# Key-value products of two linear-attention branches moved into one burst behind the first denominators

## The chip, the cores and the metric

One Trainium2 chip, one core. The metric is device microseconds of one execution; the median of several timed executions is compared. A profile is one further execution, recorded instruction by instruction.

## What is computed

```
g = sigmoid((x * gate_w).sum(-1))                   # x: 2048 x 640
for each branch (A, B), with its own wqkv, wo, 32 heads of 20:
    q, k, v = split(x_A @ wqkv)
    phi(t) = where(t > 0, t + 1, exp(t)) + 1e-6
    kv = einsum("bhsd,bhse->bhde", phi(k), v);  z = phi(k).sum(s)
    o  = (phi(q) @ kv) / (phi(q) @ z + 1e-6)
    branch = o @ wo
out = g * A + (1 - g) * B
```
Both branches read the same x. Matrix operands are bf16, sums fp32.

## The kernel before

Instead of forming v, the kernel uses that kv = phi(k)^T (x wv) = (phi(k)^T x) wv. It works in these steps.

- **Keys** (`k_both`, lines 531 to 578): 16 tiles of 128 tokens, both branches; phi is an exponential on ACT (ScalarE) and two VectorE instructions; the results PK fill the buffer FE.
- **G** (`g_unit`, 582 to 610): per branch five units of 32 matmuls, G = phi(k)^T x with the row sums z; ACT copies each to GS, a DMA transposes it into GT.
- **The m step** (`m_unit`, 622 to 656): per branch 55 small matmuls (128 rows, 64 columns of the array, at two column positions in turn) form G wv for groups of heads in one PSUM bank. Three VectorE multiplications ("masks", line 647) keep only the blocks of a head with itself and write MB.
- **W' units** (`wp_unit`, 658 to 682): kv times wo, so that value and output projections become one 640 x 640 matrix a branch. Eleven in all: five for A, five for B, and one that does the last 40 rows of both. Each is two matmuls into a pair of adjacent PSUM banks and one eviction to WS. Of A's, three evictions are on VectorE (line 680) and two on ACT; the other six are on ACT (682).
- **Rows** (`wp_store`, `wp_rows`, 684 to 698): WS goes to DRAM (wrowsA, wrowsB) and back into WPA and WPB with the rows reordered. SP issues these DMAs and those of the factors and outputs, in one queue.
- **Queries** (`q_unit`, 724 to 756): four blocks of 512 tokens, ten units each (A 0 to 4, B 0 to 4). A unit is five matmuls of 512 columns into one bank, an exponential on ACT (743), and on VectorE a min (747) and a max-and-add (752), called the two halves of a query below. They end in PQ, which lies in the same buffer FE.
- **Denominators** (`dens`, 758): phi(q) z for two blocks at once, 20 matmuls at four column positions of 32. `scale_q` (781) copies them with ACT (DN, "dn0", "dn1"), takes reciprocals on VectorE (793, "rc0", "rc1", 1.74 us each), writes them to DRAM and reads them back spread over partitions (RX), and multiplies PQ by them (811, "ML").
- **Finals** (`final`, 822): per 128 tokens and branch ten matmuls of 320 columns, PQ times WPA or WPB, joined with the gates and stored.

In the program the order is: keys; G of A; gates; G of B with A's m step after the second unit and A's W' units between the later ones; block 0 queries; B's m step; block 1 queries with the six remaining W' units between them (`WPLAG`, line 28, sets how many query units one comes later); the rows of W'; denominators 0 (blocks 0 and 1); blocks 2 and 3; denominators 2; finals.

The order on each engine is not that of the program. `_Sched.schedule` (136) is a planner that runs once, when the kernel is built. It simulates the five engines with fixed costs: a query unit 1079 ns on TensorE, halves 201 and 601 ns, `_dve_ns` (291) 380 ns for a large mask, 1740 ns for a reciprocal, and 180 to 190 ns from the end of an operation until another that depends on it may start. At each point it takes the operation that can start first; among those within 20 ns it takes the one that stands first in the program. A ready operation that stands late therefore fills any gap, and nothing is put aside for one that becomes ready a little later. The planner also assigns the eight PSUM banks, the one free longest first; a tile of two banks needs both banks of an even-odd pair (`place`, 153). On the chip every engine then runs its list strictly in order, with waits on semaphores wherever `plan` (226) finds a dependency that isn't implied by an earlier one, reuse of a bank included. Successive VectorE readers of one PSUM tile, such as the masks, count as dependent on each other (lines 103 and 115).

Of the kernel before, what the change touches and what calls it, by code (L numbers as in the profile page):

```python
# [15 lines left out]
ACT = mybir.ActivationFunctionType  # L16
# [3 lines left out]
D = 640  # L20
H = 32
DH = 20
NT = 16
NB = 4
NC = 5
EPS = 1e-6
HALF = 320
WPLAG = 2
XW = 672
# [54 lines left out]
class _Sched:  # L84
# [141 lines left out]
    def plan(self):  # L226
# [7 lines left out]
        for o in sorted(self.ops, key=lambda o: (o.start, o.idx)):  # L234
# [19 lines left out]
            for d in waits.values():  # L254
                for f in ENGINES:
                    k[f] = max(k[f], d.know[f])
            o.waits = list(lean.values())
            used.update(d for d in o.waits if d.sem is None)
# [28 lines left out]
def _act_ns(n, psum=True):  # L287
    return n / 1.2 + (52.0 if psum else 94.0)


def _dve_ns(n, rate=1):
    return n / (0.96 * rate) + 68.0
# [6 lines left out]
def bass_gated_mix__linear_attn_block__linear_attn_block__prompt_kernel(nc, A_x, A_wqkv, A_wo, B_x, B_wqkv, B_wo, gate_w, out):  # L299
# [6 lines left out]
    with ExitStack() as es:  # L306
        E = es.enter_context

        def sb(name, shape, dtype=dt.bfloat16):
            return E(nc.sbuf_tensor(name, shape, dtype))  # L310
# [13 lines left out]
        W5 = sb("W5", [128, D])  # L324
        MB = sb("MB", [128, 6, 120])
        WS = sb("WS", [120, 6, D])
# [79 lines left out]
        sch.op("POOL", lambda e: e.memset(W5[:, :], 0.0), 500, writes=[("W5", X) for X in XS], name="w5z")  # L406
        sch.op("POOL", lambda e: e.memset(MB[:, :, :], 0.0), 700, writes=[("M", q) for q in range(6)], name="mz")
        def load_x(eng, t):
# [212 lines left out]

        def m_unit(X):

            tile = _Tile(1)
            last = XS.index(X)

            def steps():
                r = []
                for q in range(6):
                    w = 12 if q < 5 else 8  # L630
                    for j in range(NC):
                        for g in (0, 1) if q < 5 else (last,):
                            at = D * j + 120 * q + 60 * g * (q < 5)
                            r.append((
                                PS[64 * g : 64 * g + 64, tile.banks[0], 60 * q : 60 * q + NC * w], WV[X][:, at : at + 64],
                                GT[X][:, j, :, 24 * q + 12 * g * (q < 5) : 24 * q + 12 * g * (q < 5) + w], j == 0, j == NC - 1, (0, 64 * g),
                            ))
                return r

            mms("m%s" % X, steps, [("GT", X, k) for k in range(NC)] + [("WV", X), ("WVP", X)], [(tile,)], 25 * 75 + 400)  # L640
            for q0, q1, g, w in ((0, 5, 0, 12), (0, 5, 1, 12), (5, 6, last, 8)):
                n = DH * (w // 4)

                def mask(e, q0=q0, q1=q1, g=g, w=w, n=n):
                    p0 = 64 * g
                    m = CB[p0 : p0 + n, C_MM : C_MM + 60].rearrange("p (k i) -> p k i", i=12)[:, :, 0:w]
                    return e.tensor_tensor(
                        out=MB[p0 : p0 + n, q0:q1, 60 * g : 60 * g + n].rearrange("p q (i k) -> p q k i", k=NC),
                        in0=PS[p0 : p0 + n, tile.banks[0], 60 * q0 : 60 * q0 + n * (q1 - q0)].rearrange("p (q k i) -> p q k i", k=NC, i=w),
                        in1=m.unsqueeze(1).to_broadcast([n, q1 - q0, NC, w]), op=ALU.mult,  # L650
                    )

                sch.op(
                    "DVE", mask, _dve_ns(n * (q1 - q0)), reads=[(tile,), ("CB",)], writes=[("M", q) for q in range(q0, q1)],
                    name="mm%s" % X,
                )

        def wp_unit(X, q):

            tile = _Tile(2)  # L660
            w = W5 if q == 5 else WO[X][:, q, :]

            def steps():
                return [
                    (PS[0:120, tile.banks[h], 0:HALF], MB[0:124, q, :], w[0:124, HALF * h : HALF * h + HALF], True, True, None)
                    for h in (0, 1)
                ]

            mms(
                "wp%s%d" % (X, q), steps, [("M", q)] + [("W5", Y) for Y in XS if q == 5] + [("WO", X, g) for g in (0, 1) if q < 5],  # L670
                [(tile,)], D + 60,
            )
            dst = WS[:, q, :].rearrange("p (h f) -> p h f", f=HALF)

            def src():
                return PS[0:120, tile.banks[0] : tile.banks[1] + 1, 0:HALF]

            name = "wpe%s%d" % (X, q)
            if X == "A" and q % 2 == 0:
                sch.op("DVE", lambda e: e.tensor_copy(dst, src()), _dve_ns(D), reads=[(tile,)], writes=[("WS", q)], name=name)  # L680
            else:
                sch.op("ACT", lambda e: e.activation(dst, src(), ACT.Copy), _act_ns(D), reads=[(tile,)], writes=[("WS", q)], name=name)

        def wp_store(X):
            dma(
                "SP", "ws" + X, WD[X].ap()[0:600, :].rearrange("(q p) f -> p q f", p=120), WS[:, 0:5, :], reads=[("WS", q) for q in range(5)],
                writes=[("WD", X, 0)], us=2.0,
            )

        def wp_rows(X):  # L690

            nat = WD[X].ap()
            p0 = 60 * XS.index(X)
            dma("SP", "ws5" + X, nat[600:D, :], WS[p0 : p0 + 40, 5, :], reads=[("WS", 5)], writes=[("WD", X, 5)], us=0.2)
            dma(
                "SP", "wp" + X, WP[X][:, :, :], nat.rearrange("(i k) f -> i k f", k=NC), reads=[("WD", X, 0), ("WD", X, 5)],
                writes=[("WP", X, k) for k in range(NC)], us=2.2,
            )
# [59 lines left out]
        def dens(b0):  # L758
# [3 lines left out]
            def den():  # L762
# [11 lines left out]

            mms(
                "den%d" % b0, den, [("ZBD", X) for X in XS] + [("PQ", X, k, b) for X in XS for k in range(NC) for b in (b0, b0 + 1)],
                [(dtile,)], 5 * 540,
            )
            return dtile

# [120 lines left out]
        gates()  # L901
        g_unit("B", 0)
        g_unit("B", 1)
        m_unit("A")
        g_unit("B", 2)
        for q in (0, 1):
            wp_unit("A", q)
        g_unit("B", 3)
        for q in (2, 3):
            wp_unit("A", q)  # L910
        g_unit("B", 4)
        wp_unit("A", 4)
        wp_store("A")
        zbd("B")
        def queries(b):
            for X in XS:
                for k in range(NC):
                    q_unit(X, b, k)
                    q = 5 * (X == "B") + k - WPLAG
                    if b == 1 and 0 <= q < 6:  # L920
                        wp_unit("B", (q - 1) % 6)
                        if q == 0:
                            wp_rows("A")

        def finals(b):
# [5 lines left out]

        queries(0)
        m_unit("B")
        queries(1)
        wp_store("B")
        wp_rows("B")
        d01 = dens(0)
        scale_q(0, d01, 2)
        queries(2)
        queries(3)  # L940
        scale_q(1, d01, 2)
        d23 = dens(2)
        finals(0)
# [38 lines left out]
```

## Time and profile before

| | us |
|---|---|
| median of three timed runs | 190.35 (190.13 to 191.41) |
| the profiled execution's own time | 190.84 |
| its span, first to last instruction | 189.5 |
| TensorE busy / VectorE / ScalarE | 186.2 / 130.2 / 76.5 |
| A's m step, B's m step start at | 79.56, 105.98 |
| first query matmul | 95.09 |
| first denominators, second denominators | 121.77, 146.59 |
| first final | 142.42 |

Times in the profile count from the start of the span. A line of a group gives source line, engine, operation, output and inputs by tile name, shapes, count, then the busy time in us and the mean duration in ns, then the idle time ahead of it and who ended it. Consecutive matmuls overlap, so the distance of their starts, not their duration, is what one costs TensorE. In the views PEld is the load of the stationary operand, DVE is VectorE, ACT is ScalarE and SPq the issue of a DMA by SP.

### The profile page before, as it was taken

The page shows a single profiled execution, that of the slowest core. Times are in us where ns is not written, and L with a number is a line of the kernel's source. Part 1 is how long each engine was busy: PE and PEld are TensorE (multiplying, and loading weights), DVE is VectorE, ACT ScalarE, POOL GpSimd, SP SyncE. Part 2 cuts the span into 40 slices and gives each one's busy share as a digit, 9 for nine tenths or more (in the row PEclk, how much of TensorE's full clock was granted, in tenths as well). Part 3 has the DMA queues.
Part 4 walks back from the last instruction along what each step waited for, and adds up shares of the span by engine and source line. Part 5 has one row for each costly group of instructions (what it writes and reads, how often), then busy time and mean ns, then how long its engine had stood idle before and what let it go on. Part 6 is the DMA issues. An engine that isn't in the chain of part 4 may idle for free.

```text
span 189.5 us, 3208 instructions
## 1 busy us (share of the span) xinstructions
PE 186.2 (98%) x1289; PEld 124.2 (66%) x1289; DVE 130.2 (69%) x275; ACT 76.5 (40%) x129; POOL 8.2 (4%) x14
## 2 busy tenths in 40 slices
PE   8999999999999999999999999999999999999995
PEld 3555555555788888888855666455556677777774
DVE  1498988898600009996179997899999959833324
ACT  2255656565311112203255478565553422332332
POOL 8900000000000000000000000000000000000000
DMA  5999799991011111111143005675000173221212
GB/s 191 289 230 193 171 390 365 355 246 42 0 35 38 35 35 38 35 35 38 35 90 107 5 22 173 162 227 171 0 0 3 50 222 91 98 72 39 73 69 69
DMA packets 31936, 21.49 MB, mean 113 GB/s; under 512 B 16818, under 2 KB 31666, under 8 KB 31922
## 3 DMA queue, kind: packets, MB, share of 16 engines
q1 hardware_dynamic: 31490, 20.80, 39.9%
q10 hardware_dynamic: 432, 0.49, 0.7%
q8 instruction: 10, 0.16, 0.4%
q14 instruction: 4, 0.03, 0.1%
HBM read 12.05 MB, written 5.31 MB: 92 GB/s over the span
## 4 chain that ended last, share of the span: by engine, by line
PE 94%; DMA 3%; SPq 1%; issue 0%; ACT 0%; DVE 0%
PE ps L383 94%; DMA WK<-in_B_wqkv_dram 3%; SPq L372 1%; ACT TS L859 0%; DVE OL L865 0%
## 5 line engine op out<-in xcount | busy, mean ns | idle before, releaser
L383 PE MATMUL ps<-WK,XT 128*128 128x512 bf16 (+2 forms) x250 | 44.2, 337 | 0.4 <-DMA WK<-in_B_wqkv_dram 0.4
L383 PE MATMUL ps<-XN,FE 128*128 128x320 bf16 x320 | 44.3, 300 | 0.0
L383 PEld LDWEIGHTS ps<-XN,FE 128*128 128x128 bf16 x320 | 37.5, 117 | 6.0
L383 PEld LDWEIGHTS ps<-WK,XT 128*128 128x128 bf16 x250 | 24.1, 98 | 19.9 <-DMA WK<-in_B_wqkv_dram 1.1
L743 ACT ACTIVATE EK<-ps 128x512 bf16<-128x512 f32 x40 | 23.9, 597 | 18.4 <-PE ps L383 17.9
L563 ACT ACTIVATE EK<-ps 128x512 bf16<-128x512 f32 (+1 forms) x42 | 21.4, 526 | 16.2 <-PE ps L383 16.2
L752 DVE SCALAR_TENSOR_TENSOR FE<-ps,EK 128x512 bf16<-128x512 f32 x40 | 26.8, 687 | 0.7
L859 ACT ACTIVATE TS<-ps,GA 128x640 f32<-128x640 f32 (+2 forms) x18 | 13.2, 734 | 29.6 <-PE ps L383 29.6
L383 PE MATMUL ps<-WPB,FE 128*128 128x320 bf16 (+1 forms) x165 | 24.7, 295 | 0.0
L383 PE MATMUL ps<-WPA,FE 128*128 128x320 bf16 (+1 forms) x165 | 24.7, 295 | 0.0
L573 DVE SCALAR_TENSOR_TENSOR FE<-ps,EK 128x512 bf16<-128x512 f32 (+1 forms) x42 | 23.9, 597 | 0.5
L865 DVE SCALAR_TENSOR_TENSOR OS<-ps,GA,TS 128x640 bf16<-128x640 f32 x15 | 13.0, 868 | 15.2 <-PE ps L383 12.8
L383 PE MATMUL ps<-XT,WQA 128*128 128x512 bf16 x100 | 22.8, 380 | 0.0
L383 PE MATMUL ps<-XT,WQB 128*128 128x512 bf16 x100 | 22.7, 379 | 0.0
L600 ACT ACTIVATE GS<-ps 128x640 bf16<-128x640 f32 x10 | 7.0, 704 | 37.1 <-PE ps L383 37.1
L383 PEld LDWEIGHTS ps<-WPA,FE 128*128 128x128 bf16 x165 | 15.9, 98 | 6.1
L383 PEld LDWEIGHTS ps<-WPB,FE 128*128 128x128 bf16 x165 | 15.8, 98 | 6.2 <-ACT TS L859 0.4
L383 PEld LDWEIGHTS ps<-XT,WQB 128*128 128x128 bf16 x100 | 11.7, 117 | 9.2
L383 PEld LDWEIGHTS ps<-XT,WQA 128*128 128x128 bf16 x100 | 11.6, 118 | 9.4 <-issue 0.4
L705 DVE SCALAR_TENSOR_TENSOR GP<-XN,GWB 128x640 bf16<-128x640 bf16 x16 | 13.2, 828 | 4.1 <-PE ps L383 3.6
L567 DVE TENSOR_SCALAR EK<-EK 128x512 bf16<-128x512 bf16 (+1 forms) x42 | 11.4, 271 | 3.1
L811 DVE TENSOR_TENSOR FE<-FE,RX 128x1280 bf16<-128x1280 bf16 (+1 forms) x20 | 12.6, 684 | 1.1 <-DMA RX<-factor 1.1
(52 smaller groups left out, 81.1 us busy)
## 6 DMA issues: line engine op xcount, KB each, us to landing
out_dram<-OS SPq DMA_DIRECT2D x15, 160.0 KB, 1.8
XN<-in_A_x_dram SPq DMA_DIRECT2D x3, 640.0 KB, 8.5
factor<-RC SPq DMA_DIRECT2D x4, 256.0 KB, 2.6
RX<-factor SPq DMA_DIRECT2D x4, 256.0 KB, 3.1
WVA<-in_A_wqkv_dram SPq DMA_DIRECT2D x1, 800.0 KB, 10.3
WQA<-in_A_wqkv_dram SPq DMA_DIRECT2D x1, 800.0 KB, 11.7
WVB<-in_B_wqkv_dram SPq DMA_DIRECT2D x1, 800.0 KB, 11.2
WQB<-in_B_wqkv_dram SPq DMA_DIRECT2D x1, 800.0 KB, 12.3
```

What stands on the lines that cost most here:

```text
L372: ins = e.dma_start(dst() if callable(dst) else dst, src() if callable(src) else src, transpose=transpose)
L383: ins = pe.matmul(o, l, r, start=a, stop=z, tile_position=tp, skip_group_check=True)
L563: "ACT", lambda e, ps=ps, ek=ek: e.activation(ek(), ps(), ACT.Exp), _act_ns(n), reads=[(tile,)], writes=[(es,)],
L567: "DVE", lambda e, ek=ek: e.tensor_scalar(ek(), ek(), 1.0, EPS, op0=ALU.min, op1=ALU.add), _dve_ns(n, 4),
L573: return e.scalar_tensor_tensor(out=out, in0=two(ps()), scalar=0.0, in1=two(ek()), op0=ALU.max, op1=ALU.add)
L600: "ACT", lambda e: e.activation(GS[:, k, :].rearrange("p (h f) -> p h f", f=HALF), pair(tile, HALF), ACT.Copy),
L705: lambda e, t=t: e.scalar_tensor_tensor(out=GP[:, :], in0=XN[:, t, 0:D], scalar=1.0, in1=GWB[:, :], op0=ALU.mult, op1=ALU.mult, accum_out= ...
L743: "ACT", lambda e: e.activation(ek(), PS[:, tile.banks[0], :], ACT.Exp), _act_ns(512), reads=[(tile,)],
L752: lambda e: e.scalar_tensor_tensor(out=dst, in0=PS[:, tile.banks[0], :], scalar=0.0, in1=ek(), op0=ALU.max, op1=ALU.add),
L811: return e.tensor_tensor(out=v, in0=v, in1=RX[:, xs.slot, 512 * x + w * j : 512 * x + w * j + w].unsqueeze(1).to_broadcast([128, NC, w]), ...
L859: "ACT", lambda e, acc=acc, t_ap=t_ap: e.activation(t_ap(), acc(), ACT.Copy, scale=GA[:, 0, t : t + 1]),
L865: lambda e, acc=acc, t_ap=t_ap, o_ap=o_ap: e.scalar_tensor_tensor(out=o_ap(), in0=acc(), scalar=GA[:, 1, t : t + 1], in1=t_ap(), op0=ALU.m ...
```

## The change

- A's and B's m steps become one operation, `m_both`, of 110 matmuls into two banks: A's and B's full groups, then the two 40-row remainders in turn. It is made to follow the first denominators on TensorE (`after`). Six masks follow; MB holds eleven groups instead of six.
- All eleven W' units stand among the queries of blocks 2 and 3, each WPLAG = 3 units after its place in the count, in the order A 0 to 4, the shared one, B 0 to 4. Their evictions are all on ACT. A's go to GS (free once G has been transposed), B's to WS.
- A's rows are stored and reloaded after the sixth W' unit, B's after the eleventh.
- `queries(2)` now stands ahead of `scale_q(0)`.
- Where an instruction waits for several others, the waits stand in the order of the planned ends.

```
-WPLAG = 2
+WPLAG = 3
...
-            o.waits = list(lean.values())
+            o.waits = sorted(lean.values(), key=lambda d: d.end)
...
-        MB = sb("MB", [128, 6, 120])
+        MB = sb("MB", [128, 11, 120])
...
-        def m_unit(X):
+        def m_both(after):
+            tiles = [_Tile(1), _Tile(1)]
+            def step(x, q, g, j):
+                w, lo = (12, 12 * g) if q < 5 else (8, 0)
+                at = D * j + 120 * q + DH * lo // 4
+                return (
+                    PS[64 * g : 64 * g + 64, tiles[x].banks[0], 60 * q : 60 * q + NC * w], WV[XS[x]][:, at : at + 64],
+                    GT[XS[x]][:, j, :, 24 * q + lo : 24 * q + lo + w], j == 0, j == NC - 1, (0, 64 * g),
+                )
             def steps():
+                r = [step(x, q, g, j) for x in (0, 1) for q in range(5) for j in range(NC) for g in (0, 1)]
+                return r + [step(x, 5, x, j) for j in range(NC) for x in (0, 1)]
+            mms(
+                "m", steps, [("GT", X, k) for X in XS for k in range(NC)] + [("WV", X) for X in XS] + [("WVP", X) for X in XS],
+                [(t,) for t in tiles], 110 * 38 + 240, after=after,
+            )
+            for x, q0, q1, g, w in ((0, 0, 5, 0, 12), (0, 0, 5, 1, 12), (0, 5, 6, 0, 8), (1, 5, 6, 1, 8), (1, 0, 5, 0, 12), (1, 0, 5, 1, 12)):
+                n = DH * (w // 4)
+                o0 = 10 if q0 == 5 else 5 * x
...
+        def ws(u):
+            return GS[0:120, u, :] if u < 5 else WS[:, u - 5, :]
+        def wp_unit(u):
...
-            if X == "A" and q % 2 == 0:
-                sch.op("DVE", lambda e: e.tensor_copy(dst, src()), _dve_ns(D), reads=[(tile,)], writes=[("WS", q)], name=name)
-            else:
-                sch.op("ACT", lambda e: e.activation(dst, src(), ACT.Copy), _act_ns(D), reads=[(tile,)], writes=[("WS", q)], name=name)
+            sch.op(
+                "ACT",
+                lambda e: e.activation(
+                    ws(u).rearrange("p (h f) -> p h f", f=HALF), PS[0:120, tile.banks[0] : tile.banks[1] + 1, 0:HALF], ACT.Copy
+                ),
+                _act_ns(D), reads=[(tile,)], writes=[("WS", u)] + [("GS", u)] * (u < 5), name="wpe%d" % u,
+            )
...
-            return dtile
+            return dtile, o
...
-        g_unit("B", 0)
-        g_unit("B", 1)
-        m_unit("A")
...
+        for k in range(NC):
+            g_unit("B", k)
         zbd("B")
+        order = [0, 1, 2, 3, 4, 10, 5, 6, 7, 8, 9]
         def queries(b):
             for X in XS:
                 for k in range(NC):
                     q_unit(X, b, k)
+                    i = 10 * (b - 2) + 5 * (X == "B") + k - WPLAG
+                    if 0 <= i < 11:
+                        wp_unit(order[i])
+                        if i == 5:
+                            wp_store("A")
                             wp_rows("A")
+                        if i == 10:
+                            wp_store("B")
+                            wp_rows("B")
...
         queries(0)
-        m_unit("B")
         queries(1)
-        wp_store("B")
-        wp_rows("B")
-        d01 = dens(0)
+        d01, den = dens(0)
+        m_both(den)
+        queries(2)
         scale_q(0, d01, 2)
-        queries(2)
         queries(3)
         scale_q(1, d01, 2)
-        d23 = dens(2)
+        d23, _ = dens(2)
```

## The prediction

> **What bounds the kernel now.** I read the page's busy line and chain first, then the chain in order of time, then busy time by stretch.
>
> ```profile
> PE 186.2 (98%) x1289; PEld 124.2 (66%) x1289; DVE 130.2 (69%) x275; ACT 76.5 (40%) x129; POOL 8.2 (4%) x14
> ```
> ```profile
> 9.17 177.87 PE ps L383 x1241
> ```
> From 9.17 to 187.04 us TensorE hands on to itself; no other engine releases it. So the end moves by what TensorE's own sequence gains or loses, and any new wait on TensorE adds in full: there is no slack ahead of it.
>
> Busy time of the engines by stretch (PE, PEld, DVE, ACT, POOL), core 0:
>
> ```profile
> 95.10:105.90 10.80, 10.80 (x52) 5.74 (x49) 9.38 (x20) 6.06 (x10) 0.00 (x0) 1.00 0.36 86
> ...
> 119.50:131.60 12.10, 12.10 (x71) 6.24 (x70) 11.26 (x21) 6.92 (x12) 0.00 (x0) 1.00 0.70 200
> 131.60:142.40 10.80, 10.80 (x51) 5.85 (x50) 10.80 (x25) 5.97 (x10) 0.00 (x0) 1.00 0.06 18
> 142.40:152.80 10.40, 10.40 (x88) 6.92 (x87) 10.40 (x15) 3.92 (x6) 0.00 (x0) 1.00 0.18 59
> ```
> Among the block-2 and 3 queries (119.5 to 142.4) VectorE is as full as TensorE. It is late there but hidden: TensorE runs ahead through the eight PSUM banks. That is the stretch into which the change puts work. The costs, by shape:
>
> ```profile
> L752 DVE SCALAR_TENSOR_TENSOR FE<-ps,EK 128x512 bf16<-128x512 f32 x40 | 26.8, 687 | 0.7
> ...
> L793 DVE RECIPROCAL RC<-DN 128x256 bf16<-128x256 f32 x4 | 7.0, 1742 | 0.1
> ...
> L682 ACT ACTIVATE WS<-ps 120x640 bf16<-120x640 f32 x8 | 5.6, 698 | 0.0
> ...
> L647 DVE TENSOR_TENSOR MB<-ps,CB 60x300 bf16<-60x300 f32 x4 | 4.1, 1030 | 0.2
> ...
> L680 DVE CAST WS<-ps 120x640 bf16<-120x640 f32 x3 | 2.5, 822 | 5.9 <-PE ps L383 5.9
> ...
> L647 DVE TENSOR_TENSOR MB<-ps,CB 40x40 bf16<-40x40 f32 x2 | 0.5, 274 | 0.1
> ```
> A large mask takes 1.03 us; the planner (which fixes every engine's order and every bank) books 0.38. Now B's m step, in order of time:
>
> ```profile
> 100.49 5.56 PE L383 MATMUL ps<-XT,WQB 128*128 128x512 bf16 x25
> ...
> 105.98 1.13 PE L383 MATMUL ps<-GTB,WVB 128*64 128x60 bf16 x55
> ...
> 107.04 2.96 PEld L383 LDWEIGHTS ps<-XT,WQA 128*128 128x128 bf16 x15
> ...
> 107.15 1.02 DVE L647 TENSOR_TENSOR MB<-ps,CB 60x300 bf16<-60x300 f32 x1
> 107.92 0.77 DVE L752 SCALAR_TENSOR_TENSOR FE<-ps,EK 128x512 bf16<-128x512 f32 x1
> ```
> 25 query matmuls 0.216 us apart (5.40 us a block half, 1.08 a unit) end at 105.89; the next query starts at 107.04. So m costs TensorE 1.15, of which 0.09 at its entry is the change of tile shape (m starts 0.31, not 0.216, after the last query). An independent instruction follows a mask after 0.77. And the first denominators:
>
> ```profile
> 121.77 0.39 PE L383 MATMUL ps<-FE,ZBDA 128*32 128x512 bf16 x2
> ...
> 122.97 3.43 PE L383 MATMUL ps<-XT,WQA 128*128 128x512 bf16 x15
> ...
> 123.59 1.75 DVE L793 RECIPROCAL RC<-DN 128x256 bf16<-128x256 f32 x1
> 125.26 0.23 DVE L747 TENSOR_SCALAR EK<-EK 128x512 bf16<-128x512 bf16 x1
> ...
> 125.41 1.74 DVE L793 RECIPROCAL RC<-DN 128x256 bf16<-128x256 f32 x1
> ```
> First denominator matmul to first query after it: 1.20; to the first reciprocal: 1.82. A reciprocal holds VectorE 1.67 (123.59 to 125.26). The planner put the second one between the two halves of a query, because that gap was free in its plan: it fills gaps without looking ahead. This matters below.
>
> **TensorE's own work.** Removed: A's m step (79.56 to 80.61 plus 0.09 at entry, 1.15) and B's (1.15): 2.30. Added: one burst of 110 matmuls. In the trace two column halves start together and such pairs follow every 0.032; the five last ones (one half only) take 0.032 each. The burst pairs everything: 55 pairs, 1.78, plus 0.12 to the next query. Its entry switch replaces that from the denominators to queries (0.31 in either case). So 1.90, a gain of 0.40; the trace's one slow gap of 0.03 behind each switch back goes once more: **0.45**. The eleven W' units keep their price: 117.08 to 117.36 is 0.28, wherever they stand. Bounds: 0.35 (no pairing gain) to 0.55 (no drain between the two column shapes).
>
> [...]
>
> **What moves with it.** Without m and five W' units in A's share (1.15 + 5 x 0.27 = 2.5) queries start at 92.6 instead of 95.1; block 0 and 1 lose 1.15 + 6 x 0.28 more, so the denominators start 26.7 - 2.85 later, at D = 116.4. With eighteen query units, burst and eleven W' units behind D, TensorE would be through the queries at 142.0 (before: 142.4). VectorE loses three W' evictions (3 x 0.82), all from a stretch where it had room (9.6 of 15.6 us busy from 79.5 to 95.1); worth nothing. ACT gains them: a query plus a W' eviction is 0.60 + 0.70 against 1.36 of TensorE, and the rows of 111 to 118 show ACT keeping up at just that mix. [...] The sum takes ACT.
>
> The larger zero fill of MB (0.70 x 11/6 = 1.28 on POOL near 7 us) delays two fills that nothing needs before 52 us: nothing. Sorted waits: the trace has 25 separate wait records of 51 ns on TensorE's queue, under cover today. At most three waits will really be late, so within 0.15 either way; I take 0.
>
> **The new wait.** Six masks now stand behind D instead of at 81 and 107: VectorE has no slack there. The order follows from the planner's own costs (used for order only; times are the trace's). Its mask chain is serial with 0.18 us between links, so rc1 fills the first gap: rc0, mask 1, rc1, mask 2, then masks 3 to 6 among the query halves. With the trace's steps, in us behind D: rc0 1.82, mask 1 3.49, rc1 4.26, mask 2 5.92 to 6.96, mask 3 to 7.28, mask 6 9.5 to 10.5; the block-2 query halves of A,2 and A,3 stand in between, and A,4 follows, done at 11.3.
>
> TensorE meanwhile: burst 1.19, queries A2, A3, A4, B0 from 3.07, the first W' unit at 7.4. It needs masks 1 to 3 (bank and data): 7.28, just in time, 0 to 0.1. But a W' unit needs a whole pair of adjacent banks. By the planner's rotation the third one (10.1) takes the pair of A,3 and A,4, which it believes free 0.2 earlier; the trace's masks, 4 x 0.65 longer, free it at 11.3. Restart included: **1.35 us of waiting**. Other bank assignments give 0 (a pair freed by ACT) to 2.1 (masks strictly back to back). I take 1.35, as the masks' 2.6 us less the margins met. After it TensorE is as late as VectorE, and nothing further up to the last query (143.5).
>
> **The tail.** Two waits end there. WPB: rows of the DMA issues,
>
> ```profile
> WPB<-wrowsB SPq DMA_DIRECT2D x1, 800.0 KB, 4.4
> ...
> wrowsB<-WS SPq DMA_DIRECT2D x1, 750.0 KB, 4.9
> ```
> The last W' unit ends about 137.0, its eviction about 138.2: store and load make 9.3, WPB is there at 147.6 (before: landed at 127.8, first used at 143.78). A's store moves from 97.06 to about 131.5 on SP, behind both factor pairs, so no factor waits for it; its rows and WPA's load follow it (5.2 and 4.3), WPA lands near 141. B's store, rows and load come next, and their waits hold up only output rows not yet made. A's W' rows lie in GS now, free since the last transpose (95.8 + 2.6). TensorE has A's rows of tiles 0 and 1 (2 x 1.36, to 146.2) and the second denominators (1.2) to do first: 147.5. The denominators themselves wait for the last query half, 2.5 to 4.5 behind the last query (now 145.5 - 142.4 = 3.1) against 2.7 of cover. Together 0 to 1.5; I take **0.3**, as both lie at the edge of cover.
>
> Sum: -0.45 + 1.35 + 0.3 = +1.2. The profiled execution (span 189.5, time 190.84, which is 0.49 above the median) would be 192.0; the median 190.35 becomes **191.5**.
>
> **Rivals.**
> Banks suffice: no wait, 190.35 - 0.45 = 189.9. For it: before, VectorE ended 3.1 us behind TensorE and no wait showed. Against: then no bank pair was asked for among block 2 and 3.
> Slower: VectorE's lag outlasts PSUM. One mechanism: masks and both reciprocals (5.0 + 3.3 us) in a run leave some seven query units unserved; if these plus a W' pair exceed eight banks more than once, each later pair waits too. With 2.1 at the burst and 1.5 at the tail: 190.35 - 0.45 + 3.6 = 193.5. It decides from 2.4 us of waiting in all. For it: 10.80 of 10.80 busy. Against: each W' unit lends VectorE 0.28 of recovery.
> The change doesn't merge the switches (waits between denominators and burst): GT is long landed (95.8 + 2.6), so hardly; 190.4.
>
> **Chances.** One wait of 1 to 2 us (190.6 to 192.2): 0.45. No wait (189.8 to 190.6, with the unmerged case): 0.27. Above 192.25: 0.25. Something that frees more than 1.9: 0.03. A difference under 1% (1.9 us) is about what can't be told from no change. Hence faster 0.03, same 0.45 + 0.27 = 0.72, slower 0.25. Range: the bounds -0.55 and +3.0, 189.8 to 193.4; the likeliest case alone 190.6 to 192.2.
>
> **What would show it.** Right: 110 small matmuls in about 1.8 us behind the denominators; a reciprocal between the first two masks; TensorE idle over 1 us before the third W' unit, ended by VectorE's second half of a query (line 752 of before); last query near 143.5. Wrong: TensorE's chain unbroken and last query at 142.0 (rival one); repeated gaps of TensorE between 120 and 140 (rival two); first use of WPB late by more than 1.5, or the burst at 2.7.

## The result, and the profile after

| | before | after | ratio |
|---|---|---|---|
| median of the timed runs (lowest to highest) | 190.99 (190.13 to 191.41) | 196.38 (195.07 to 197.73) | 1.028 [1.023, 1.034] |
| profiled execution, its span | 190.84, 189.5 | 196.96, 195.6 | |

Slower by 2.8%, outside the range of the prediction (189.8 to 193.4). The views are read in the order of those shown for before. First the busy line and the shares of the chain, from the page of after:

```profile
PE 188.0 (96%) x1289; PEld 124.7 (64%) x1289; DVE 129.4 (66%) x272; ACT 78.3 (40%) x132; POOL 8.7 (4%) x14
...
PE 81%; DMA 9%; DVE 6%; SPq 1%; ACT 1%; issue 1%; ACTq 0%; DVEq 0%
```

TensorE no longer hands on only to itself: DMA and VectorE stand in the chain. Who stopped it is in the view of waits (waiting engine and line, releaser, us in all, times, longest):

```profile
PE ps L383 <- DMA WPB<-wrowsB: 2.4, 1, 2.4
PE ps L383 <- DVE FE L758: 1.9, 1, 1.9
...
PEld ps L383 <- DMA WPA<-wrowsA: 0.5, 1, 0.5
...
PE ps L383 <- DVE MB L649: 0.2, 1, 0.2
```

Two single waits. The first one, in the timeline behind the denominators (lines 649, 758 and 799 are 647, 752 and 793 of before):

```profile
117.26 0.98 PE L383 MATMUL ps<-GTA,WVA 128*64 128x60 bf16 x50
...
117.89 1.75 DVE L799 RECIPROCAL RC<-DN 128x256 bf16<-128x256 f32 x1
...
119.11 3.43 PE L383 MATMUL ps<-XT,WQA 128*128 128x512 bf16 x15
...
119.56 0.96 DVE L649 TENSOR_TENSOR MB<-ps,CB 60x300 bf16<-60x300 f32 x1
...
120.27 1.70 DVE L799 RECIPROCAL RC<-DN 128x256 bf16<-128x256 f32 x1
...
122.00 1.04 DVE L649 TENSOR_TENSOR MB<-ps,CB 60x300 bf16<-60x300 f32 x1
...
123.79 0.45 PE L383 MATMUL ps<-WOA,MB 124*120 124x320 bf16 x2 [0.16 <-DVE MB L649]
...
126.26 1.01 DVE L649 TENSOR_TENSOR MB<-ps,CB 60x300 bf16<-60x300 f32 x1
...
127.81 1.29 DVE L758 SCALAR_TENSOR_TENSOR FE<-ps,EK 128x512 bf16<-128x512 f32 x2
...
128.56 0.48 PE L383 MATMUL ps<-WOA,MB 124*120 124x320 bf16 x2 [1.88 <-DVE FE L758]
```

The burst starts at 117.26, the next query at 119.11. A reciprocal stands between the first two masks, the sixth mask ends at 127.27, the query half whose bank the third W' unit needs (the second half of A,4) ends at 128.50, and TensorE starts the unit at 128.56. The bracket counts 1.88 us idle; by the starts of the matmuls, which is what counts for TensorE, the wait is 2.04. A smaller one of 0.33 stands ahead of the first W' unit (at 123.79). The second wait, in the timeline of the tail:

```profile
138.32 0.35 SPq L372 DMA_DIRECT2D WPA<-wrowsA  x1
...
138.71 0.43 SPq L372 DMA_DIRECT2D wrowsB<-WS  x1
...
146.35 0.35 SPq L372 DMA_DIRECT2D WPB<-wrowsB  x1
...
150.73 4.43 PE L383 MATMUL ps<-WPB,FE 128*128 128x320 bf16 x20 [2.43 <-DMA WPB<-wrowsB]
```

B's rows leave 0.39 us after the load of A's and take 7.6 us until SP goes on; the load takes 4.2 more. TensorE had ended the second denominators and stood still for 2.5. The third loss is in the windows (us; busy time of PE, PEld, DVE, ACT, POOL; granted clock; DMA share; GB/s):

```profile
119.00:129.00 10.00, 7.96 (x49) 4.40 (x44) 9.82 (x16) 4.88 (x8) 0.00 (x0) 1.00 0.38 107
...
144.00:150.70 6.70, 4.27 (x41) 2.32 (x41) 4.12 (x6) 3.13 (x5) 0.00 (x0) 1.00 0.52 180
150.70:156.50 5.80, 5.77 (x31) 3.67 (x32) 2.19 (x3) 0.00 (x0) 0.00 (x0) 0.71 0.25 76
```

TensorE is busy 7.96 of 10.00 and 4.27 of 6.70 where it waits, and behind the second wait its granted clock is 0.71. The trace has the clock at one half from 151.872 for 3.413 us; WPB matmuls stand 267 ns apart there and 136 before and after it. That is 1.7 us lost. Three of the six executions have the lowered mean clock (196.95 to 197.73), three have not (195.07 to 195.81).

The account closes. From the first denominators to the last matmul: before 121.77 to 187.14, 65.4; after 116.07 to 193.10, 77.0. The burst (1.85 up to the next query) and eleven W' units (0.275 each) moved behind the denominators explain 4.9. The other 6.8 (from unrounded figures) are the waits of 0.33, 2.04, 0.19 (first use of WPA) and 2.50 and the 1.7 at half clock.

### The profile page after: what moved, and what is told of

Same layout as the page of the kernel before. It is cut to its first block, busy times and chain, and to the rows that moved or that the text cites. A ratio compares the mean times of both kernels' runs of the same rounds, so it can differ in the third digit from the quotient of the medians.

```text
span 195.6 us, 3206 instructions
## 1 busy us (share of the span) xinstructions
PE 188.0 (96%) x1289; PEld 124.7 (64%) x1289; DVE 129.4 (66%) x272; ACT 78.3 (40%) x132; POOL 8.7 (4%) x14
## 4 chain that ended last, share of the span: by engine, by line
PE 81%; DMA 9%; DVE 6%; SPq 1%; ACT 1%; issue 1%; ACTq 0%; DVEq 0%
PE ps L383 81%; DMA wrowsB<-WS 4%; DMA WK<-in_B_wqkv_dram 3%; DVE MB L649 2%; DMA WPB<-wrowsB 2%; DVE RC L799 2%; DVE FE L758 1%; SPq L372 1%; DVE EK L753 1%; ACT EK L749 1%; ACT WS L683 0%; ACT TS L865 0%; DVE OL L871 0%; ACTq L276 0%; DVEq L276 0%
## 5 line engine op out<-in xcount | busy, mean ns | idle before, releaser
L383 PE MATMUL ps<-XN,FE 128*128 128x320 bf16 x320 | 43.8, 300 | 0.0
L383 PE MATMUL ps<-WPB,FE 128*128 128x320 bf16 (+1 forms) x165 | 26.1, 307 | 2.4 <-DMA WPB<-wrowsB 2.4
L758 DVE SCALAR_TENSOR_TENSOR FE<-ps,EK 128x512 bf16<-128x512 f32 x40 | 27.4, 691 | 0.9
L383 PEld LDWEIGHTS ps<-WPB,FE 128*128 128x128 bf16 x165 | 16.4, 101 | 9.5 <-issue 2.9
L567 DVE TENSOR_SCALAR EK<-EK 128x512 bf16<-128x512 bf16 (+1 forms) x42 | 11.3, 270 | 2.8
## 6 DMA issues: line engine op xcount, KB each, us to landing
WVB<-in_B_wqkv_dram SPq DMA_DIRECT2D x1, 800.0 KB, 11.2
```

The source lines that it names most:

```text
L383: ins = pe.matmul(o, l, r, start=a, stop=z, tile_position=tp, skip_group_check=True)
L567: "DVE", lambda e, ek=ek: e.tensor_scalar(ek(), ek(), 1.0, EPS, op0=ALU.min, op1=ALU.add), _dve_ns(n, 4),
L758: lambda e: e.scalar_tensor_tensor(out=dst, in0=PS[:, tile.banks[0], :], scalar=0.0, in1=ek(), op0=ALU.max, op1=ALU.add),
```

## The theory, its rivals and the experiments

The theory: the change costs what TensorE waits for. It has two roots. The 2.1 us of A's two large masks (and rc1 between them) land where VectorE has no room, and the W' rows come so late that they are stored while another transfer is in flight. The rivals: the need for a pair of banks, ScalarE's sole evictions, the sorted waits, the merged burst itself, or the place beside the reciprocals for any mask at all.

All times in the second column are medians. The columns "rest", "waits" and "half clock" are read from the one profiled execution of each kernel: "rest" is the time from the first denominators to the last matmul less 65.4 and less the 4.9 of moved work, so what is left to explain. "Waits" are those of TensorE, up to the last query and behind it. "Low" counts the executions with a mean clock under 0.995.

| kernel | us (lowest to highest) | ratio to before | rest | waits among queries | behind | half clock | low |
|---|---|---|---|---|---|---|---|
| after | 196.38 (195.07 to 197.73) | 1.028 [1.023, 1.034] | 6.8 | 0.33 + 2.04 | 0.19 + 2.50 | 1.7 | 3 of 6 |
| second reciprocal last | 192.26 (191.83 to 192.77) | 1.008 [1.006, 1.010] | 1.9 | 0.44 + 0.49 + 0.39 | 0.29 + 0.23 + 0.11 | | 0 of 4 |
| WPA loaded early | 192.88 (192.88 to 194.98) | 1.014 [1.010, 1.018] | 4.3 | 0.33 + 2.06 | 0.20 | 1.7 | 1 of 4 |
| filled wait | 195.46 (195.06 to 197.12) | 1.026 [1.023, 1.029] | 5.2 | 0.33 + 2.06 | 2.7, filled | | 1 of 6 |
| burst between blocks | 192.57 (192.32 to 192.99) | 1.010 [1.008, 1.011] | 2.3 | 1.05 | 0.68 + 0.24 + 0.16 | | 0 of 6 |
| waits unsorted | 197.59 (196.47 to 198.85) | 1.038 [1.032, 1.044] | 8.4 | 0.24 + 2.11 | 2.57 | 2 x 1.7 | 4 of 4 |
| masks priced | 194.94 (194.34 to 197.25) | 1.026 [1.019, 1.032] | 6.6 | 0.15 + 0.28 + 0.90 | 3.10 | 1.7 | 1 of 4 |
| evictions shared | 195.14 (194.80 to 195.41) | 1.024 [1.023, 1.026] | 4.9 | 0.33 + 1.92 + 0.13 + 0.88 | 0.48 + 1.10 | | 0 of 4 |
| only B moved | 192.24 (192.04 to 192.42) | 1.008 [1.006, 1.010] | 1.5 | 0.41 + 0.32 + 0.73 | 0 | | 0 of 4 |
| two masks left out | 191.38 (190.61 to 191.75) | 1.003 [1.001, 1.004] | 0.9 | 0.64 + 0.15 | 0.08 | | 0 of 10 |
| single banks | 194.39 (193.56 to 195.07) | 1.019 [1.015, 1.023] | 4.8 | 0.97 + 1.12 + 0.91 | 0.20 | 1.7 | 2 of 4 |
| both orders mended | 191.88 (191.26 to 192.37) | 1.005 [1.004, 1.007] | 1.5 | 0.14 | 1.37 | | 0 of 8 |
| rows in two parts | 192.84 (192.68 to 193.00) | 1.011 [1.009, 1.014] | 2.4 | 0.14 | 2.29 | | 0 of 6 |
| finals in due order | 191.51 (191.03 to 192.42) | 1.004 [1.003, 1.006] | 1.1 | 0.14 | 0.98 | | 0 of 12 |

The row "burst between blocks" is counted from the first query, with the work moved there; "only B moved" with B's m step and six W' units as the moved work. In every row the waits and the half clock make the rest, to within 0.2 us (0.4 for masks priced). So hardly anything else costs TensorE time there, and each experiment can be read wait by wait.

**The second reciprocal behind the masks**: it is made to follow the sixth one.

```
...
-        m_both(den)
+        masked = m_both(den)
...
-        scale_q(1, d01, 2)
+        scale_q(1, d01, 2, masked)
```

> The changed kernel with one wait added: the second reciprocal comes after the sixth mask instead of between the first two. Theory one (TensorE's two waits before W' units come from masks held up by rc1): mask 2 ends 1.7 us earlier, the 0.33 us wait before the first W' unit goes, the 1.96 us wait before the third shrinks to 0.3 or less, so the last query ends 1.7 to 2.2 us earlier behind the first denominators. B's rows come earlier by the same, so the 2.5 us wait for WPB and the clock drop stay: about 194.5. Rival (VectorE has too much work here in any order): the waits move to later units, the sum of TensorE's waits up to the last query stays near 2.3 us, time near 196.4.

192.26, lower than expected, because the tail went too. The waits among the queries became three of 0.39 to 0.49: 1.32 in all instead of 2.37, between the 0.3 of the theory and the 2.3 of the rival. A's rows left SP 3.9 us earlier, and B's left 1.8 us behind A's load. SP in the timeline of this kernel:

```profile
135.60 0.35 SPq L372 DMA_DIRECT2D WPA<-wrowsA  x1
...
137.40 0.33 SPq L372 DMA_DIRECT2D wrowsB<-WS  x1
...
142.72 0.35 SPq L372 DMA_DIRECT2D WPB<-wrowsB  x1
```

The store took 5.3 instead of 7.6. So the planner's place for one reciprocal is worth some 4 us: 1.0 through the waits among the queries, 2.1 through what these did to the rows, and the rest, as far as it can be told, through the clock.

**WPA loaded early.** WPA is filled at the start from wo, so A's half of the output isn't the product W'; the traffic at the tail is B's alone.

```
+        dma("SP", "wpA", WP["A"][:, :, :], wo["A"].rearrange(...), ...)
...
         def wp_rows(X):
...
+            if X == "A":
+                return
...
```

> The changed kernel, but WPA is loaded at the start, from wo instead of A's rows; A's rows are still stored. The output therefore has wrong A parts. Theory one (the store of B's rows is slow because A's load runs beside it): store 4.9 us instead of 7.6, WPB 2.5 to 2.8 us earlier, first use of WPB almost without a wait, no clock drop behind it; 196.4 becomes 191.8 to 192.5. Rival (the store is slow from its place among the factor DMAs and the queries, or the B chain is simply too long): store stays near 7, wait near 2.5 us, time 195 to 196.5.

192.88, slightly above the expected range. B's store was issued at 140.90 with no load of A's rows ahead of it and took 4.9 again, and the wait for WPB was 0.2. From the DMA issues (KB, us to landing) of after, then of this kernel:

```profile
wrowsB<-WS SPq DMA_DIRECT2D x1, 750.0 KB, 7.6
...
wrowsB<-WS SPq DMA_DIRECT2D x1, 750.0 KB, 4.9
```

The collision is shown: with the same late W' units, the load of A's rows in flight is what made 2.7 us of the store's 7.6. In the profiled execution the half clock came behind the first wait this time (granted clock is the number ahead of the DMA share):

```profile
130.20:133.70 3.50, 3.50 (x12) 1.70 (x10) 3.50 (x8) 1.51 (x4) 0.00 (x0) 0.51 0.00 0
```

**The wait for WPB filled** with eleven matmuls on constants, whose result nobody reads.

```
-        d23, _ = dens(2)
+        d23, den2 = dens(2)
+        for _ in range(11):
+            fill = mms("fill", ..., after=fill)
```

> The changed kernel plus 11 matmuls of 512 columns on a constant (2.4 us at full clock, result unused) right behind the second denominators, where TensorE waits 2.5 us for WPB. Theory one (the clock falls to 0.71 over 5.8 us because TensorE stood idle 2.8 us): the clock stays at 1.0 in every run, WPB arrives when it did, time 194.8 to 195.3 against 196.4, and never above 196. Rival (the drop comes from elsewhere, a power or thermal limit): drops still occur in about half of the runs, median near 196.4 or above it.

195.46, just above the expected range; WPB came as late as in after (first used at 150.86), and five of six executions kept the full clock. The sixth, at 197.12, was above what was expected of any; the wait of 2.06 among the queries stays in this kernel and can have done it, but that execution has no profile. That idleness costs clock here is supported; that the tail's wait alone does it is not.

**The burst between blocks 0 and 1**, all W' units ten query units earlier.

```
-                    i = 10 * (b - 2) + 5 * (X == "B") + k - WPLAG
+                    i = 10 * (b - 1) + 5 * (X == "B") + k - WPLAG
...
         queries(0)
+        m_both(at[0])
         queries(1)
         d01, den = dens(0)
-        m_both(den)
```

> The changed kernel with the one burst moved between the queries of blocks 0 and 1 and the eleven W' units ten query units earlier, among blocks 1 and 2. Theory one (the burst itself gains 0.45 us on TensorE, the loss is only its place next to two reciprocals and the lateness of the rows): no wait of TensorE above 0.3 us, WPB landed over 5 us before its first use, 0.3 to 0.6 us below the kernel before. Rival (W' units need bank pairs that VectorE's lag denies wherever they stand in the queries): 1 to 2 us above the kernel before.

192.57: my expectation failed and the rival held. WPB was there in time, yet 1.05 us went ahead of the second W' unit (VectorE ran five masks in a row), 0.68 at the first final, and the rest in two small waits.

```profile
105.16 3.77 DVE L649 TENSOR_TENSOR MB<-ps,CB 60x300 bf16<-60x300 f32 x5
...
111.80 0.48 PE L383 MATMUL ps<-WOA,MB 124*120 124x320 bf16 x2 [0.88 <-DVE FE L758]
```

In the planner's orders the masks cost in this place too, not only beside the reciprocals.

**The waits in the old order.**

```
-            o.waits = sorted(lean.values(), key=lambda d: d.end)
+            o.waits = list(lean.values())
```

> The changed kernel with the waits of an instruction in their old order; every engine's list of instructions is the same. Theory one (the order of waits matters only where one is late, by 0.05 us): TensorE's waits of 0.3, 2.0 and 2.5 us stay within 0.1, time 195.1 without a clock drop and 197 with one, as for the changed kernel. Rival (the sorting moves when DMAs are issued or VectorE starts): over 0.5 us of difference in one of these waits.

The waits of TensorE are those of after within 0.15. The two executions with one clock drop (196.47, 196.68) compare with the three of after that had one (196.95 to 197.73); the other two had two drops (198.50, 198.85). The order of the waits has no cost of its own here. Whether it has a part in how often the clock drops can't be told from four executions.

**Masks at their measured price** in the planner.

```
-                    "DVE", mask, _dve_ns(n * (q1 - q0)), ...
+                    "DVE", mask, 1030 if q1 - q0 == 5 else 274, ...
```

> The changed kernel, but the planner books 1.03 and 0.27 us for the masks, as measured, instead of 0.38 and 0.11. It now puts the W' units later and more of them side by side. Theory one (TensorE's waits up to the last query come from the planner believing bank pairs free that are not): these waits fall from 2.3 us to 0.5 or less; the last W' unit comes no earlier, so the rows of B are as late and the wait for WPB stays 1.5 to 2.5; 192.5 to 194.5. Rival (VectorE's work is too much in any order): the sum of waits up to the last query stays above 1.5 us.

194.94, above what was expected. The wait of 2.04 is gone (1.33 among the queries in all), but W' units bunch up and one waits 0.90 for an eviction by ScalarE, so that B's rows again leave 0.39 us behind A's load, take 7.5, and WPB is waited for 3.1 us. A repair of the first wait alone brings little while the collision stays: the three executions at full clock took 194.34 to 195.12, against 195.07 to 195.81 in after.

**A's first, third and fifth eviction on VectorE.**

```
+            if u in (0, 2, 4):
+                sch.op("DVE", lambda e: e.tensor_copy(...), _dve_ns(D), ...)
+                return
```

> The changed kernel with the first, third and fifth W' evictions of A on VectorE again (0.82 us each), as before the change. Theory one (VectorE is the full engine between the denominators and the last query): 2.5 us more on VectorE, TensorE's waits up to the last query grow by 1 to 2.5, time 196 to 198.5. Rival (ACT alone with the evictions holds the bank pairs): waits shrink, time 193 to 195.

The waits among the queries grew by 0.9 (3.26 instead of 2.37), nearly the 1 to 2.5 expected; the time did not, since the wait for WPB shrank as TensorE came later, and none of the four executions had the half clock. ScalarE as sole evictor was not the loss.

**A's two large masks left out**, so that A's W' and with it A's part of the output are not computed.

```
+                if x == 0 and q0 == 0:
+                    continue
```

> The changed kernel without A's two large masks (2.1 us of VectorE work left out; A's W' rows are then zero except the shared ones, so the output is wrong). All W' units and DMAs stay. Theory one (the masks that came from a stretch where VectorE had room are what TensorE waits for): no wait above 0.5 us up to the last query, B's rows about 2 us earlier, 191 to 192.5. Rival (the bank pairs are short because of the eleven W' units themselves): waits up to the last query stay at 1.5 us or more, time above 194.

191.38. With 2.1 us less on VectorE the waits among the queries fall from 2.37 to 0.79 (one of 0.64, where none above 0.5 was expected) and the tail's to 0.08. So without A's masks in this stretch most of the waiting goes; whether it is their amount or their order this run can't tell, the run with both orders mended can.

**Only B moved**, made from before: B's m step, B's five W' units and the shared one stand behind the denominators, A's stay.

```
-        m_unit("B")
         queries(1)
...
+        d01, den = dens(0)
+        m_unit("B", den)
+        queries(2)
```

> The kernel before with one half of the change: A's m step, masks and W' units stay in the G stage; B's m step follows the first denominators and its six W' units stand among the queries of block 2 and 3. Theory one (what costs is VectorE work moved out of a stretch with room, which is A's half): VectorE has no more to do from the first query on than before, TensorE's waits up to the last query 0.7 us or less together, WPB in time, 190.3 to 191.5. Rival (the place behind the denominators, beside two reciprocals, is what costs, for either half): waits of 1.5 us or more, above 192.

192.24, so the expected range was missed and the rival came closer. With half the masks the waits still sum to 1.46. The timeline shows why:

```profile
120.50 1.75 DVE L793 RECIPROCAL RC<-DN 128x256 bf16<-128x256 f32 x1
...
122.17 0.97 DVE L647 TENSOR_TENSOR MB<-ps,CB 60x300 bf16<-60x300 f32 x1
...
122.89 1.69 DVE L793 RECIPROCAL RC<-DN 128x256 bf16<-128x256 f32 x1
...
124.61 1.02 DVE L647 TENSOR_TENSOR MB<-ps,CB 60x300 bf16<-60x300 f32 x1
```

The same order as in after, a mask, the second reciprocal, a mask: the first W' unit needs both masks and waits for the reciprocal between them. The place beside the reciprocals has a price for either half.

**W' units in two tiles of one bank** instead of a pair.

```
-            tile = _Tile(2)
+            half = [_Tile(1), _Tile(1)]
...
```

> The changed kernel with each W' unit in two tiles of one bank, each evicted by itself (22 ACT evictions of 320 columns instead of 11 of 640, about 2 us more on ACT in all). Theory one in its narrow form (the long wait comes from needing an even-odd pair): the wait before the third unit falls from 2.0 us below 1.0, as its first half can take any free bank; total waits up to the last query 1 us or less, the wait for WPB stays near 2.5 or more with ACT's extra work; 194 to 196. Rival (VectorE is late and any bank would be waited for): waits up to the last query stay near 2.3 us, 195 to 197.

194.39, within the time expected by the theory and below the rival's, but the waits say otherwise. Without a pair to ask for, those among the queries were 0.97, 1.12 and 0.91, 3.0 in all, and all of them end with VectorE. The pair decides where TensorE stops, not how long: the rival (any bank is late, because VectorE is) held. The wait for WPB, expected at 2.5 or more, was 0.20. B's store, 2.2 us behind A's load, took 5.2.

**Both orders mended**: the second reciprocal last and the masks at their price.

```
-                    "DVE", mask, _dve_ns(n * (q1 - q0)), ...
+                    "DVE", mask, 1030 if q1 - q0 == 5 else 274, ...
...
-        scale_q(1, d01, 2)
+        scale_q(1, d01, 2, masked)
```

> The changed kernel with the second reciprocal after the sixth mask and the masks priced as measured in the planner: both causes of the waits before W' units removed, the work unchanged. Theory one: waits up to the last query from 1.3 us (with the reciprocal alone) to 0.5 or less, wait for WPB 0 to 1; 190.5 to 192. Rival (VectorE's 2.3 us of extra work come out at the end of the queries instead): a wait of 1 us or more for the last query halves before the finals or the second denominators, 192 to 193.5.

191.88. The waits among the queries are down to 0.14, and from the denominators to the last query it takes 25.5, as the prediction had it without waits (142.0 less 116.4 is 25.6). VectorE does the same work as in after and is still nearly full (busy 25.54 of the 26.00 us from 116 to 142, TensorE 25.71), so it was the order and not the amount of its work that made 2.2 of the 2.37 us. What remains is 1.37 for WPB, more than the 0 to 1 expected; B's store, 1.5 us behind A's load, took 6.3.

```profile
147.37 2.88 PE L383 MATMUL ps<-WPB,FE 128*128 128x320 bf16 x20 [1.30 <-ACT DN L794]
```

The bracket names ScalarE's copy of the second denominators, which ended at 147.23. In the planner's list this matmul waits for two things only: the eviction of the first final by ScalarE, done at 144.35, and WPB, which landed at 147.24. So the wait is for WPB.

**Rows stored and loaded in two parts**, on top of that: three groups, then the rest.

```
-                        if i == 5:
-                            wp_store("A")
-                            wp_rows("A")
+                        if i in (2, 5):
+                            wp_store("A", i // 5)
+                            wp_rows("A", i // 5)
...
```

> The run with both orders mended (second reciprocal after the masks, masks priced as measured), and the rows of W' stored and reloaded in two parts (groups 0 to 2, then 3, 4 and the last 40 rows), so that after the last W' unit only 240 rows of B have to go out and 280 to come back. Theory one (what is left of the loss is the 1.37 us wait for WPB): store and load of the second part together 6 to 7 us instead of 10.7, wait for WPB 0.3 us or less, the 0.45 us of the burst shows: 190.3 to 190.8, 0.1 to 0.5 below the kernel before. Rival (other costs behind it, VectorE's extra masks foremost, surface as the next wait): 191.3 to 192.

192.84. WPB was first used at 145.8, 1.6 earlier, though the second part's store and load took 9.0 (from 136.81) instead of 6 to 7. But the planner booked the parts cheaper than they are and set the first use of WPB ahead of the second denominators: TensorE stood for 2.29 in front of it. The expectation failed through an order, again.

**The finals in due order**: the same with the planner's prices of these DMAs raised, so that four tiles of A and the second denominators come first. The cut is against after; in "rows in two parts" the prices were 0.4 a group and 1.2.

```
-            writes=[("WD", X, 0)], us=2.0,
+            writes=[("WD", X, part)], us=0.9 * (q1 - q0),
...
-            us=2.2,
+            us=3.0,
```

> The kernel with both orders mended and the rows moved in two parts, with one thing more: the planner books the store at 0.9 us per group and each load at 3.0 us (before: 0.3 to 0.4 and 2.2), so that on TensorE A's first two tiles, the second denominators and A's next two tiles all stand ahead of the first use of WPB. Theory (what the change costs is two waits of TensorE, for the masks and for WPB, and nothing else): both are gone, the wait for WPB is 0 to 0.3 us, and the gain of the burst of some 0.45 shows at last: 190.3 to 191.2 against 190.7 of the kernel before. Rival (VectorE's 2.1 us of extra work among the queries is due later all the same, as waits on evictions or reciprocals among the finals): 191.5 to 192.5, with single waits of TensorE behind the second denominators.

191.51, at the rival's edge. The wait for WPB is gone, and a new one of 0.98 stands five microseconds later:

```profile
146.18 3.37 DVE L804 RECIPROCAL RC<-DN 128x256 bf16<-128x256 f32 x2 [2.50 <-ACT DN L798]
...
149.47 2.96 DVE L822 TENSOR_TENSOR FE<-FE,RX 128x1280 bf16<-128x1280 bf16 x4
...
152.34 2.46 DVE L876 SCALAR_TENSOR_TENSOR OS<-ps,GA,TS 128x640 bf16<-128x640 f32 x3
...
153.28 0.99 PE L383 MATMUL ps<-WPB,FE 128*128 128x320 bf16 x6 [0.81 <-DVE OS L876]
```

Behind the second denominators VectorE does both reciprocals and four scalings without a pause; the joins of the finals (OS), which free their banks, come after them, and TensorE runs out of banks. How much of the 0.98 is VectorE's added work and how much the new order of the finals was not separated. No version came out faster than before.

Of the theory's two roots the late rows stand; the first is narrower than it was put, since the order of VectorE's work made those waits and not the lack of room. Of the rivals, the place beside the reciprocals holds as far as the planner's order goes ("only B moved"); the pair of banks, ScalarE's evictions, the sorted waits and the burst itself cost nothing that these runs show.

## Why the prediction was wrong, point by point

The forecast was +1.2 us, the medians give +5.4 (190.99 to 196.38; the forecast started from 190.35, the median of three). For the profiled executions (190.84 and 196.96, +6.1) the terms are: TensorE's own work -0.45 as foretold; waits among the queries 2.37 instead of 1.35; waits of the tail 2.69 instead of 0.3; half clock 1.7 instead of nothing. They make +6.3.

- **TensorE's own gain: right.** The burst took 1.85 up to the next query (1.90 foretold). No run shows the 2.7 that the prediction names for a burst that would prove it wrong. That the gain is real shows in the sums: with 0.14 us of waits, "both orders mended" needs 25.5 from denominators to last query.
- **The places: right.** Queries start at 92.2 (92.6 foretold), denominators at 116.1 (116.4), and VectorE's order is the one foretold, rc0, mask 1, rc1, mask 2, then the rest among query halves. The third W' unit is the one that waits, ended by a second query half; last query 143.8 (143.5).
- **The bank wait: the mechanism right, the size short.** 1.35 foretold, 2.04 measured, and 0.33 instead of 0 to 0.1 ahead of the first unit. Mask 2 ended within 0.01 us of the foretold time; then the query halves among the masks took 0.7 more than was counted (mask 6 ended 11.2 behind the denominators instead of 10.5), and behind mask 6 two mins went ahead of A,4's second half (1.23 instead of 0.8), which ended at 12.4 instead of 11.3. The upper bound that the prediction named, 2.1, was the better number.
- **The tail: the step that failed most.** "Store and load make 9.3" summed the two from a row where the store had the queue for itself; here it took 7.6 and the load 4.2. WPB came at 150.7 instead of 147.6, with 2.5 of waiting instead of 0.3. The prediction had the order on SP right, but priced B's store as if alone, though by its own times A's load (136.7 to 141) was in flight when that store left (138.2). Of the 3.0 us by which WPB landed late (150.59), 2.7 are the store and 0.5 its later start (138.71 instead of 138.2); the load took 0.2 less than the row of before. The bound of 1.5 didn't take that in either.
- **The clock: not in the sum at all.** 1.7 us behind a wait of over 2 us, in half of the executions.
- **The range was too narrow by its own terms.** Its upper end of +3.0 lies below the sum of the bounds named (-0.35 + 2.1 + 1.5 = 3.25) and leaves out the slower rival's 193.5.
- **The slower rival** had the mechanism (VectorE's lag) and the deciding point, 2.4 us of waiting in all; 5.1 were measured. Its 193.5 lacked the collision and the clock. "Banks suffice" and "not merged" are refuted by the profile.
- **The sorted waits and ScalarE's evictions** were both taken at nothing. In after no wait of TensorE ends with ScalarE, and the old order of the waits leaves those of TensorE the same within 0.15. In another order ScalarE can be the one waited for (0.90 in "masks priced").

## What to carry to other kernels

Work that moves between stages is priced by the room of the engine that must finish it, here VectorE, not by the engine that gains; look whether the new stage has slack on every engine, and what a greedy planner will put between two dependent instructions: with the order mended, the same VectorE work left 0.14 of 2.37 us of waiting among the queries. A DMA is priced from a row where its neighbours in time are the same: one that follows another directly on the queue can cost half as much again, as B's rows did here (7.6 us, 0.39 behind A's load, against 4.9). Where a forecast leaves a wait of 2 us in a row on TensorE, the clock belongs in the range as well: of the six kernels here with a wait of 2.0 to 3.1 us, 10 of 30 executions had the lowered clock, at 1.7 us for each drop.

## What the runs showed of the hardware

**Half clock behind short waits.** In after's profile the drop among the matmuls lasts 3.413 us at one half and begins 1.15 us after TensorE resumes from the wait of 2.50 us. In "WPA loaded early" (granted clock 0.87 from 128.00 to 131.00, 0.51 from 130.20 to 133.70) it begins 1.1 us after the wait of 2.06. In "single banks" it stands among waits of 0.97, 1.12 and 0.91 within 3.5 us: five query matmuls from 127.47 take 2.33 us there, 1.24 elsewhere. Of the kernels with such waits some executions have it and some not: 3 of 6, 1 of 4, 1 of 6, 4 of 4, 1 of 4, 2 of 4, and 0 of 6 for "rows in two parts" with its 2.29. No execution of another kernel had it; their waits were under 1.4, or 1.92 in "evictions shared".

In after's trace the clock changes on one grid: it is granted in full from 5.099, at one half from 151.872, which is 43 times 3.413 us later, and at one half again, behind the last matmul, from 196.245, 13 times 3.413 us after the first drop. Counted along this grid, TensorE stood idle for 2.27 us in the stretch ahead of the first drop and for 2.91 in the one ahead of the second. The grid cuts the wait among the queries in two, 1.30 and 0.58 us, and no drop follows either; no other stretch has more than 0.17. In "WPA loaded early" the wait, 1.90 by its bracket, lies whole within the 3.413 us ahead of the drop. Between 1.30 and 1.90 these two traces show nothing, and why the 2.29 of "rows in two parts" cost no clock was not shown.

**A store beside a load.** The 750 KB of B's rows took from issue to landing, by how long after A's 800 KB load they were issued: 7.6 us (0.39 behind), 6.3 (1.5), 5.2 (1.8), 5.2 (2.2), 4.9 (no load of A). The load isn't the only neighbour that counts: in "burst between blocks" the store left 3.9 behind it, with a factor issued 0.39 after the store, and took 5.9. A's load itself took 5.8 next to it, against 4.2 for B's, which was alone.

**Small matmuls at 16 ns.** The 110 of the burst start within 1.73 us, in pairs 0.032 us apart, one at each column position: 16 ns for each. For one position alone the row is another: the last five matmuls of B's m step in before, all in one position, stand 0.032 us apart.
